# One token difference for both mixings on GpSimd, another order of snapshots and blocks 21 and 12, a low word read unsigned, and the w_k sums on VectorE

## The chip, the cores and the metric

The kernel runs on one core of a Trainium2 chip. The metric is the device time of one execution in microseconds, the median of three runs: 1744.05 us before (1743.65 to 1745.59).

## What is computed

A Fourier transform over tokens and features, of which the real part goes on, then a channel-mixing layer in which each token is mixed with the one before it, then a two-matrix layer with a tanh. All inputs are float32, the weights are handed in as 64-bit floats.

```python
X = np.fft.fft(np.fft.fft(x, axis=1), axis=2).real      # x: 4 x 3072 x 256
x_prev = concat([zeros, X[:, :-1]], axis=1)
xk = mu_k * X + (1.0 - mu_k) * x_prev
xr = mu_r * X + (1.0 - mu_r) * x_prev
k = np.maximum(xk @ w_k, 0.0)                           # 256 x 1024
v = k * k @ w_v                                         # 1024 x 256
r = 1.0 / (1.0 + np.exp(-(xr @ w_r)))
y = r * v
h = y @ w_in                                            # 256 x 2048
return (h - np.tanh(h)) @ w_out                         # 2048 x 256
```

## The kernel before

**Three stages.** `fft_phase` makes the transform of four batches and leaves it in the tiles y (two for each batch). Meanwhile it works through a list of small closures, three or four for each step, which turn the weights from 64-bit words into float32 with integer operations on VectorE (`convert`: 17 pieces here). Then `phase1` (12 passes of two 512-token tiles) computes the first layer, and `phase2` (12 passes) the second.

**Products.** A product is three matmuls of 512 columns (`mm3`): high by high, high by low, low by high, so each operand is a pair: a high half (a cast on ScalarE) and a low half (a subtraction). `split` writes such a pair. A Winograd-like scheme makes a 2x2 block product from seven products.

**A quad.** `quad` is the unit of both phases. A pass of phase 1 has four quads (n the pass, q the quad), one of phase 2 eight. In a quad TensorE makes seven left products (a11, a12, s2, s3, s1, a22, s4) in three PSUM banks X, Z and W. ScalarE copies X out three times on the way: the snapshots s1, s2, s3. From the sums come four blocks 11, 22, 21 and 12. Each goes through `bend` (relu on ScalarE, in phase 2 tanh), `gate` (on VectorE), `hi` (cast on ScalarE) and `lo` (subtraction on VectorE), and is then the moving operand of the second products (`second`, six matmuls for a block). Blocks 11 and 22 are finished in their own quad. Blocks 21 and 12 wait in `late`, and their nine steps run in the quad after it, as do the second products of all four blocks. In phase 1 a quad has 7 x 3 + 4 x 6 matmuls and 6 more for the gate r (`r_block`), 51 in all; in phase 2 it has 45. At the end of a pass `done` multiplies the four results by r on VectorE.

**Slots.** Each quad calls `fill` four times. A call runs the closures that stand in the table `slots` under the next number, so a pass of phase 1 has 16 slots. In them the inputs of the next pass are made: `mixed` builds xk and xr for four half tiles each, with a scaled copy on ScalarE (line 502) and a multiply-add on VectorE (line 504); `left` forms four sums on GpSimd (lines 485 to 488) and splits seven operands (cast on ScalarE, subtraction on GpSimd, lines 304 and 305). Eight pieces of w_out are converted in the slots from 88 on: seven VectorE instructions, a GpSimd sum and two DMAs each. Every engine runs its instructions in the order in which they are written, so an instruction that waits holds up all that stand behind it on its engine.

**w_k.** For the four pieces of w_k `quad_weights` casts on VectorE, subtracts the low halves on GpSimd, and forms four 128 x 128 sums t on GpSimd; a second cast on VectorE waits for these.

Of the kernel before, what the change touches and what calls it, by code (L numbers as in the profile page):

```python
# [9 lines left out]
I32 = mybir.dt.int32  # L10
PSUM = bass.MemoryType.PSUM
# [240 lines left out]
NP = 12  # L252
# [30 lines left out]
class Kernel:  # L283
# [24 lines left out]
    def convert(self, rows, done, room, add, fine=False):  # L308

        V = self.V  # L310
        ALU = mybir.AluOpType
        t = {}
        def load():
            t["raw"], t["more"] = room()
            for c, r in enumerate(rows):
                n = 512 // len(rows)
                self.nc.sync.dma_start(out=t["raw"][:, n * c:n * c + n, :].rearrange("p n t -> p (n t)"), in_=r)
        def step(k, j):
            if k == j == 0:
# [3 lines left out]
            ai, bi, si = (x.bitcast(I32) for x in (a, b, s))  # L323
# [12 lines left out]
            if k == 3:  # L336
                V.scalar_tensor_tensor(b, bi, 2.0 ** -51, s, op0=ALU.mult, op1=ALU.mult)
        steps = [lambda k=k, j=j: step(k, j) for k, j in ((0, 0), (0, 1), (1, 0), (1, 1), (2, 0), (2, 1))] if fine else [lambda k=k: (step(k, 0), step(k, 1)) for k in range(3)]
        return [load] + steps + [lambda: step(3, 0)], [lambda: add.tensor_add(t["a"], t["a"], t["b"])] + [lambda f=f: f(t["a"]) for f in done]

# [20 lines left out]
    def quad_weights(self, pool, out, first=None):  # L361

        t = []
        def sums(src):
            t.append(pool.tile([128, 4, 128], F32, tag="t4", name="t4"))
            b12, b11, b21, b22 = (src[:, 128 * k:128 * k + 128] for k in range(4))
            self.split(out[:, :, 0:3], src[:, 128:512].rearrange("p (k n) -> p k n", k=3), self.G, first)
            D = self.G
            D.tensor_sub(t[0][:, 0], b12, b11)
            D.tensor_sub(t[0][:, 2], b22, b12)  # L370
            D.tensor_sub(t[0][:, 1], b22, t[0][:, 0])
            D.tensor_sub(t[0][:, 3], b21, t[0][:, 1])
# [16 lines left out]
    def quad(self, ph, n, q, nq, S, W, w2, done, extra=None):  # L389
# [10 lines left out]
        ctile = lambda: self.act.tile([128, TOK], F32, tag="c", name="c", bufs=6)  # L400
# [12 lines left out]
        late = iter(p["late"] if p else ())  # L413
        def after(k):
            for _ in range(k):
                next(late, lambda: None)()
        self.odd ^= 1
        X, Z = bank(f"x{self.odd}", "x"), bank("z", "z")
        P(X, "a11", True)
# [6 lines left out]
        after(2)  # L426
        P(X, "s2", False)
        V.tensor_add(Z, Z, s1)  # L428
        after(1)
# [8 lines left out]
        r = extra(bank(f"x{1 - self.odd}", "r")) if extra else None  # L438
# [3 lines left out]
        self.fill()  # L442
        Wb = bank("w", "w")
        P(Wb, "s1", True)
        if r:
            r()
# [6 lines left out]
        self.second(p, "21")  # L453
        lo("22", Z)
        self.fill()
# [8 lines left out]
        def t12():  # L464
            st["t12"] = bend(st["c12"])
        late = [t21, c12, lambda: gate(X, X, st["t21"]),  # L466
                t12, lambda: hi("21", X), lambda: gate(st["c12"], st["c12"], st["t12"]),  # L467
                lambda: lo("21", X), lambda: hi("12", st["c12"]),
                lambda: lo("12", st["c12"])]
        self.pend = dict(n=n, q=q, nq=nq, m=M, w=w2, done=done, late=late)  # L470


    def unit(self, S, name, src, tag="S"):
        def f():
            pool, bufs = (self.sp, 11) if tag == "S" else (self.p2b, 3)
            S[name] = pool.tile([128, 2, TOK], F32R, tag=tag, name=name, bufs=bufs)
            self.split(S[name], src(), self.G)
        return f

    def left(self, S, raw, tag="S"):  # L480

        G = self.G
        u = {k: self.unit(S, k, lambda i=i: raw[i], "S" if k in ("a11", "a12", "a22", "s1") else tag)
# [47 lines left out]
    def k_tasks(self, n):  # L531
# [6 lines left out]
        return [get(j) for j in range(4)], self.left(self.S[n], raw)  # L538

    def r_task(self, n, t, c):  # L540
        st = []
        def f0():
            st.append(self.sp.tile([128, TOK], F32, tag="xt", name="xt", bufs=2))
            self.mixed(st[0], n, t, c, 1, 0)
        def f1():
            self.mixed(st[0], n, t, c, 1, 1)
        def f2():
            if c == 0:
                self.XR[n, t] = self.xp.tile([128, 2, 2, TOK], F32R, tag="xr", name="xr", bufs=2)
            self.split(self.XR[n, t][:, :, c], st[0], self.G if n + t else self.V)  # L550
        return [f0, f1, f2]

    def phase1(self):
# [26 lines left out]
        at = self.at  # L580
        for q in range(8):
            steps, out = self.convert(self.chunk_rows(self.w_out, (q, q + 8)), self.keep(12 + q), self.y_room, self.G, True)
            z = 91 + 11 * q
            at(z - 3, steps[0])
            at(z, *steps[1:], *out)
        for n in range(NP):
            z = 16 * n
            last = n + 1 == NP
            at(z if last else z + 4, *r_task(n, 1, 0))
            at(z + 1 if last else z + 6, *r_task(n, 1, 1))  # L590
            if n % 6 == 2:
                at(z + 8, lambda n=n: self.swap_rows(block(n, 1)[0]))
            if not last:
                get, u = self.k_tasks(n + 1)
                k = z + 1 if n else z + 2
                at(k, *get[0], u["a11"])
                at(k + 2, *get[1], u["a12"])
                at(k + 4, *get[3], u["a22"])
                at(k + 6, *get[2], u["+s1"], u["s1"])
                at(z + 10 if n else z + 11, u["+s3"], u["+s2"], u["+s4"], u["s3"], u["s2"], u["s4"])  # L600
                at(z + 10, *r_task(n + 1, 0, 0))
                at(z + 12, *r_task(n + 1, 0, 1))
                if n % 6 == 1:
                    at(z + 14, lambda n=n: self.swap_rows(block(n + 1, 0)[0]))
# [8 lines left out]
    def open2(self):  # L613
# [6 lines left out]
        for q in range(3):  # L620
            self.weights2(16 * NP - 12 + 4 * q, q, self.sp, "xt", 2)
# [34 lines left out]
    def phase2(self):  # L656
# [13 lines left out]
        for n in range(NP):  # L670
            for q in range(8):
                if n == 0 and q == 1:
                    self.xctx.close()
                    self.p2b = self.ctx.enter_context(self.tc.tile_pool(name="p2b", bufs=1, side="right", reuse_waits="tile"))
                    for j in range(3, 8):
                        self.weights2(z0 + 4 * (j - 2), j, self.sp, "xt", 2)
# [6 lines left out]
        for f in self.pend["late"]:  # L683
            f()
# [82 lines left out]
```

## Time and profile before

| | before |
|---|---|
| median of three runs | 1744.05 us |
| the profiled execution's own time | 1742.07 us |
| its span, first to last instruction | 1740.3 us |
| mean granted TensorE clock | 0.995 |
| TensorE busy (matmuls) | 1693.5 us, 97% |
| VectorE, ScalarE, GpSimd busy | 1335.9, 1191.9, 490.6 us |
| first matmul of phase 1, of phase 2 | 158.24 us, 747.53 us |

Matmuls are pipelined, so two that follow each other overlap in the record; how long a stretch takes is better read from how many matmuls were issued in it. An engine's busy share is an average over the stages.

### The profile page before, as it was taken

Reading aid. Unit: us, or ns where it says so; the run is one execution under the profiler, and the core shown is the slowest. Engines: PE = TensorE matmul, PEld = TensorE weight load, DVE = VectorE, ACT = ScalarE, POOL = GpSimd, SP = SyncE. Lnnn points to the kernel's source line nnn. Section 1 sums busy time; section 2 is a strip of 40 time slices with the busy share of each in tenths; the row PEclk is TensorE's granted clock in tenths of the full one; section 3 lists DMA queues with packets and bytes.
Section 4 is the critical chain, followed back from the end, with each engine's and each line's share of the span. In section 5 each row is a group of like instructions: output and inputs, shape, how many; then the busy total and the mean of one; then the engine's idle time right before and its main releaser. Section 6 shows DMA issues by size and latency. Waiting matters only on the chain.

```text
span 1740.3 us, 22465 instructions
## 1 busy us (share of the span) xinstructions
PE 1693.5 (97%) x7962; PEld 1408.9 (81%) x7962; DVE 1335.9 (77%) x2089; ACT 1191.9 (68%) x2368; POOL 490.6 (28%) x405
## 2 busy tenths in 40 slices
PE   9998999999999999999999999999999999999999
PEld 8897788888777777887888888888888888888887
DVE  6996788888888889776777777777777777777776
ACT  6657777777777677777666666666666666666665
POOL 0214444344344453557021111202020302021100
PEclk9999999999999999999999999999999999999999
DMA  9531000001111011221101010110101010101000
GB/s 338 171 94 43 1 25 26 25 24 37 43 43 62 19 43 43 91 80 31 49 1 49 1 49 8 42 42 8 49 1 49 1 49 1 49 1 49 1 25 25
DMA packets 37441, 77.64 MB, mean 45 GB/s; under 512 B 4288, under 2 KB 11072, under 8 KB 36176
## 3 DMA queue, kind: packets, MB, share of 16 engines
q1 hardware_dynamic: 37184, 76.21, 13.2%
q8 instruction: 62, 1.02, 0.2%
q14 instruction: 51, 0.42, 0.1%
q10 hardware_dynamic: 144, 0.00, 0.0%
HBM read 45.73 MB, written 30.46 MB: 44 GB/s over the span
## 4 chain that ended last, share of the span: by engine, by line
PE 68%; DVE 17%; ACT 8%; issue 3%; DMA 2%; POOL 1%; SPq 0%; DVEq 0%; ACTq 0%; POOLq 0%
PE o L272 12%; PE o L273 12%; PE o L271 12%; PE x L271 6%; PE x L272 6%; PE x L273 6%; PE w L273 3%; PE w L271 3%; PE w L272 3%; DVE m L411 3%; ACT c L404 2%; DVE xt L504 2%; ACT m L409 1%; PE z L273 1%; PE z L272 1%
## 5 line engine op out<-in xcount | busy, mean ns | idle before, releaser
L411 DVE TENSOR_TENSOR m<-z,m 128x512 fp32r<-128x512 f32 x288 | 199.1, 691 | 184.4 <-ACT m L409 184.4
L272 PE MATMUL o<-m,WO 128*128 128x512 f32 x768 | 298.9, 389 | 0.0
L273 PE MATMUL o<-m,WO 128*128 128x512 f32 x768 | 298.8, 389 | 0.0
L271 PE MATMUL o<-m,WO 128*128 128x512 f32 x768 | 298.8, 389 | 0.0
L409 ACT CAST m<-z 128x512 fp32r<-128x512 f32 x288 | 168.9, 586 | 165.2 <-DVE z L435 84.1
L305 POOL TENSOR_TENSOR a<-xk,a 128x512 fp32r<-128x512 f32 x72 | 95.4, 1326 | 640.1 <-ACT a L304 560.3
L404 ACT ACTIVATE c<-z 128x512 f32<-128x512 f32 x288 | 172.9, 600 | 132.5 <-DVE z L447 126.0
L305 POOL TENSOR_TENSOR s<-xk,s 128x512 fp32r<-128x512 f32 x96 | 128.7, 1342 | 243.5 <-ACT s L304 243.5
L272 PEld LDWEIGHTS o<-m,WO 128*128 128x128 f32 x768 | 144.2, 188 | 30.3 <-DVE m L411 0.3
L271 PEld LDWEIGHTS o<-m,WO 128*128 128x128 f32 x768 | 144.2, 188 | 29.9
L273 PEld LDWEIGHTS o<-m,WO 128*128 128x128 f32 x768 | 144.2, 188 | 29.9
L451 DVE TENSOR_TENSOR z<-z,c 128x512 f32<-128x512 f32 x144 | 100.3, 697 | 68.8 <-ACT c L404 68.8
L271 PE MATMUL o<-m,wv 128*128 128x512 f32 x384 | 149.6, 390 | 0.0
L273 PE MATMUL o<-m,wv 128*128 128x512 f32 x384 | 149.4, 389 | 0.0
L272 PE MATMUL o<-m,wv 128*128 128x512 f32 x384 | 149.4, 389 | 0.0
L422 ACT COPY s<-x 128x512 f32<-128x512 f32 x144 | 84.5, 587 | 73.2 <-PE x L273 73.0
L447 DVE TENSOR_TENSOR z<-w,s 128x512 f32<-128x512 f32 x144 | 100.5, 698 | 23.2 <-ACT r L569 5.8
L435 DVE TENSOR_TENSOR z<-z,c 128x512 f32<-128x512 f32 x144 | 100.5, 698 | 21.6 <-ACT c L404 19.5
L467 DVE TENSOR_TENSOR c<-c 128x512 f32<-128x512 f32 x96 | 71.2, 741 | 52.8 <-ACT c L404 52.8
L466 DVE TENSOR_TENSOR x<-x,c 128x512 f32<-128x512 f32 x144 | 99.1, 688 | 2.6 <-ACT c L404 2.6
L431 ACT COPY s<-x 128x512 f32<-128x512 f32 x144 | 84.6, 588 | 22.3 <-PE x L273 22.2
L428 DVE TENSOR_TENSOR z<-z,s 128x512 f32<-128x512 f32 x144 | 99.0, 688 | 0.0
(174 smaller groups left out, 4219.0 us busy)
## 6 DMA issues: line engine op xcount, KB each, us to landing
spill<-r SPq DMA_DIRECT2D x48, 256.0 KB
xk<-spill SPq DMA_DIRECT2D x48, 256.0 KB
out<-o SPq DMA_DIRECT2D x22, 512.0 KB
xr<-x SPq DMA_DIRECT2D x9, 1024.0 KB
raw<-w_in SPq DMA_DIRECT2D x32, 128.0 KB
cv<-w_out SPq DMA_DIRECT2D x16, 256.0 KB
wf<-wf SPq DMA_DIRECT2D x16, 256.0 KB
wf<-cva SPq DMA_DIRECT2D x12, 256.0 KB
```

Source lines behind the costliest of these rows:

```text
L271: T.matmul(ps, w[0], m[0], start=start, stop=False, skip_group_check=True)
L272: T.matmul(ps, w[0], m[1], start=False, stop=False, skip_group_check=True)
L273: T.matmul(ps, w[1], m[0], start=False, stop=stop, skip_group_check=True)
L305: eng.tensor_sub(out[:, 1], src, out[:, 0].bitcast(F32))
L404: A.activation(t, src, ACT.Tanh if ph == 2 else ACT.Relu)
L409: A.copy(M[blk][:, 0], g)
L411: V.tensor_sub(M[blk][:, 1], g, M[blk][:, 0].bitcast(F32))
L428: V.tensor_add(Z, Z, s1)
L435: gate(Z, Z, t11)
L447: V.tensor_add(Z, Wb, s3)
L451: gate(Z, Z, t22)
L466: late = [t21, c12, lambda: gate(X, X, st["t21"]), t12, lambda: hi("21", X), lambda: gate(st["c12"], st["c12"], st["t12"]), lambda: lo("21 ...
```

## The change

Four things change.

First, the mixing. Before, xk and xr of a half tile each took a scaled copy and a multiply-add, four instructions. Now (`both_tasks`) GpSimd forms one difference d = X - x_prev, VectorE makes xk = mu_k d + x_prev, ScalarE scales d by mu_r in place, and GpSimd adds x_prev to give xr. A dictionary says in which of the 16 slots each step stands (d, k, m, +, x for difference, xk, scaling, sum and split of half tile 0 to 3). The inputs of pass 0 keep the old way, but their sums and low halves go to VectorE.

Second, the quad of phase 1. The snapshot s2 is copied before block 12's relu and cast, block 21's second products come before the product s1, and block 12's after it. Phase 2 keeps its order.

Third, `convert` multiplies the low word straight as an unsigned integer, without the shift by one bit ahead of it. The w_out pieces are spread over 48 chosen slots of passes 6 to 9.

Fourth, the sums t of w_k are formed on VectorE. Buffers: c tiles 4 in place of 6, xt tiles 4 in place of 2.

```diff
-            if (k, j) == (2, 1):
-                V.tensor_scalar(bi, low, 1, None, op0=ALU.logical_shift_right)
             if k == 3:
-                V.scalar_tensor_tensor(b, bi, 2.0 ** -51, s, op0=ALU.mult, op1=ALU.mult)
+                V.scalar_tensor_tensor(b, low.bitcast(U32), 2.0 ** -52, s, op0=ALU.mult, op1=ALU.mult)
...
-            D = self.G
-            D.tensor_sub(t[0][:, 0], b12, b11)
+            eng.tensor_sub(t[0][:, 0], b12, b11)
...
         P(X, "a11", True)
-        after(3)
+        if ph == 1:
+            late("t21", "g21")
...
         s1 = stile()
         A.copy(s1, X)
-        after(3)
+        if ph == 1:
+            late("c12", "h21")
...
         A.copy(s2, X)
+        if ph == 1:
+            self.fill()
+            late("t12", "g12")
         t11 = bend(Z)
-        self.fill()
...
         gate(Z, Z, t11)
+        if ph == 1:
+            late("h12", "l12")
         P(X, "s3", False)
...
+        if ph == 1:
+            self.second(p, "21")
         Wb = bank("w", "w")
         P(Wb, "s1", True)
...
         hi("22", Z)
-        self.second(p, "21")
-        lo("22", Z)
-        self.fill()
+        if ph == 1:
+            self.fill()
+            lo("22", Z)
...
+                self.G.tensor_sub(d[j], t[:, cu:cu + TOK], y[j])
...
+                self.V.scalar_tensor_tensor(raw[j], d[j], self.mut[:, j % 2:j % 2 + 1], y[j], op0=ALU.mult, op1=ALU.add)
...
+            u[f"m{j}"] = lambda j=j: self.A.activation(d[j], d[j], ACT.Copy, scale=self.mut[:, 2 + j % 2:3 + j % 2])
+            u[f"+{j}"] = lambda j=j: self.G.tensor_add(d[j], d[j], y[j])
+            u[f"x{j}"] = lambda j=j: self.r_parts(n, j // 2, j % 2, d[j])
...
+        free = iter([16 * n + k for n in range(6, NP) for k in (0, 2, 3, 6, 7, 9, 10, 11, 12, 13, 14, 15)])
...
+                for k, names in {0: "d0", 1: "k0 d1", 3: "m0", 4: "k1 d3 a11", 5: "k3 +0", 6: "m1 d2 a12", 7: "+1", 8: "k2 m3 a22",
+                                 9: "+s1 m2", 10: "+3 s1 +s3", 11: "+s2 +2", 12: "s3 +s4", 13: "s2", 14: "s4", 15: "x0", 16: "x1", 18: "x2", 19: "x3"}.items():
```

How the instructions stand on the engines at three places:

VectorE in the transform stage, around the third piece of w_k, before (L333, L335 and L337 are the last three steps of `convert`, L304 the casts into TK, L217 and L219 write y).

```order
L339 TENSOR_TENSOR cva<-cva,cvb 128x512
L304 CAST TK<-cva 128x384
L217 TENSOR_TENSOR y_1_770<-pe,pq 128x12x16
L219 SCALAR_TENSOR_TENSOR y_1_770<-pq,cst,pe 128x12x16
L217 TENSOR_TENSOR y_1_771<-pe,pq 128x12x16
L219 SCALAR_TENSOR_TENSOR y_1_771<-pq,cst,pe 128x12x16
L333 TENSOR_SCALAR cvs<-cva 128x512
L335 TENSOR_SCALAR cvb<-raw 128x512
L337 SCALAR_TENSOR_TENSOR cvb<-cvb,cvs 128x512
```

The same place in the changed kernel.

```order
L338 TENSOR_TENSOR cva<-cva,cvb 128x512
L305 CAST TK<-cva 128x384
L367 TENSOR_TENSOR t_912<-cva 128x128
L368 TENSOR_TENSOR t_912<-cva 128x128
L369 TENSOR_TENSOR t_912<-cva,t_912 128x128
L370 TENSOR_TENSOR t_912<-cva,t_912 128x128
L218 TENSOR_TENSOR y_1_764<-pe,pq 128x12x16
```

The four sums now stand on VectorE right behind the cast; one of the three last steps of `convert` is gone everywhere.

ScalarE in phase 1, between two quads of pass 3, before (c the relus, m the high halves, L422 and L431 the snapshots s1 and s2, c<-w and m<-w those of block 12).

```order
L409 CAST m_3274<-z 128x512
L304 CAST a_3284<-xk 128x512
L502 ACTIVATE xk<-y_1_771,omu 128x512
L404 ACTIVATE c<-x 128x512
L422 COPY s<-x 128x512
L404 ACTIVATE c<-w 128x512
L409 CAST m_3308<-x 128x512
L409 CAST m_3321<-w 128x512
L431 COPY s<-x 128x512
```

The changed kernel, from the first to the second quad of pass 3 (L598 is m0, L424 and L439 the snapshots).

```order
L402 ACTIVATE c<-z 128x512
L305 CAST xr<-xt 128x512
L407 CAST m_3161<-z 128x512
L305 CAST xr<-xt 128x512
L598 ACTIVATE xt<-xt,mut 128x512
L402 ACTIVATE c<-x 128x512
L424 COPY s<-x 128x512
L407 CAST m_3184<-x 128x512
L439 COPY s<-x 128x512
```

Ahead of the snapshot s2 stand one relu and one high half fewer; ahead of block 21's relu stand the high half of block 22, a cast of xr and m0.

VectorE in the changed kernel, first quad of pass 2 (L593 is k0, L611 the products with r, L464 and L468 sum and gate of block 22, L409 low halves).

```order
L409 TENSOR_TENSOR m_2677<-z,m_2677 128x512
L593 SCALAR_TENSOR_TENSOR xk<-xt,mut,y_0_341 128x512
L611 TENSOR_TENSOR r<-o_2346,r 128x512
L611 TENSOR_TENSOR r<-o_2347,r 128x512
L464 TENSOR_TENSOR z<-w,s 128x512
L611 TENSOR_TENSOR r<-o_2316,r 128x512
L611 TENSOR_TENSOR r<-o_2317,r 128x512
L468 TENSOR_TENSOR z<-z,c 128x512
L409 TENSOR_TENSOR m_2726<-z,m_2726 128x512
```

GpSimd at the same place: the split of xr (x0 and x1), d0 and d1, then x2 and x3.

```order
L306 TENSOR_TENSOR xr<-xt,xr 128x512 x2
L588 TENSOR_TENSOR xt<-y_0_341 128x512
L588 TENSOR_TENSOR xt<-y_0_340 128x512
L306 TENSOR_TENSOR xr<-xt,xr 128x512 x2
```

Two of the four products with r, and k0, now stand ahead of the sum of block 22, and d1 follows d0 on GpSimd without a wait between them.

## Rows read from the trace of the kernel before

**Rows 1.** The page, part 1: busy time of each engine.

```profile
PE 1693.5 (97%) x7962; PEld 1408.9 (81%) x7962; DVE 1335.9 (77%) x2089; ACT 1191.9 (68%) x2368; POOL 490.6 (28%) x405
```

**Rows 2.** Windows: stretch, length, busy time (instructions) by engine, granted clock, DMA.

```profile
158.20:205.00 46.80, 38.67 (x162) 28.96 (x161) 33.80 (x53) 34.64 (x65) 20.51 (x16) 1.00 0.04 12
205.00:428.00 223.00, 221.15 (x969) 181.18 (x968) 181.31 (x268) 172.74 (x319) 92.25 (x71) 1.00 0.08 27
428.00:703.00 275.00, 257.46 (x1098) 204.79 (x1097) 238.32 (x355) 197.23 (x362) 126.22 (x92) 0.99 0.12 40
...
900.00:1000.00 100.00, 100.00 (x442) 82.80 (x442) 72.94 (x111) 64.57 (x118) 14.44 (x12) 1.00 0.07 22
```

**Rows 3.** Waits, 428 to 703 us: who waited for whom, us, times, longest.

```profile
PE x L271 <- ACT s L431: 16.5, 13, 2.2
```

**Rows 4.** VectorE's and ScalarE's timelines, quads of pass 3: start, us, instruction [idle before].

```profile
326.22 1.80 DVE L504 SCALAR_TENSOR_TENSOR xt<-y,mut,xt 128x512 f32<-128x512 f32 x1
...
330.51 0.59 ACT L431 COPY s<-x 128x512 f32<-128x512 f32 x1
...
336.26 0.73 ACT L502 ACTIVATE xt<-y,omu 128x512 f32<-128x512 f32 x1
...
344.98 0.69 DVE L411 TENSOR_TENSOR m<-z,m 128x512 fp32r<-128x512 f32 x1 [0.91 <-ACT m L409]
345.58 0.74 DVE L504 SCALAR_TENSOR_TENSOR xt<-y,mut,xt 128x512 f32<-128x512 f32 x1
346.24 0.69 DVE L447 TENSOR_TENSOR z<-w,s 128x512 f32<-128x512 f32 x1
347.60 0.70 DVE L451 TENSOR_TENSOR z<-z,c 128x512 f32<-128x512 f32 x1 [0.67 <-ACT c L404]
349.11 0.69 DVE L411 TENSOR_TENSOR m<-z,m 128x512 fp32r<-128x512 f32 x1 [0.81 <-ACT m L409]
```

**Rows 5.** GpSimd's timeline, same stretch.

```profile
326.17 1.30 POOL L305 TENSOR_TENSOR a<-xk,a 128x512 fp32r<-128x512 f32 x1 [0.40 <-ACT a L304]
```

**Rows 6.** TensorE's timeline, same stretch.

```profile
331.15 0.50 PE L271 MATMUL x<-s,TK 128*128 128x512 f32 x1 [0.37 <-ACT s L431]
...
345.39 0.39 PE L273 MATMUL w<-s,TK 128*128 128x512 f32 x1
...
351.74 0.39 PE L271 MATMUL z<-a,TK 128*128 128x512 f32 x1
```

**Rows 7.** Windows of the transform stage, same columns.

```profile
50.00:60.00 10.00, 10.00 (x91) 9.74 (x90) 9.83 (x20) 7.03 (x30) 0.60 (x1) 1.00 0.69 229
...
110.00:120.00 10.00, 6.67 (x48) 6.42 (x48) 9.76 (x24) 4.00 (x17) 1.16 (x1) 0.84 0.30 96
120.00:130.00 10.00, 10.00 (x76) 10.00 (x76) 9.72 (x23) 5.70 (x24) 1.27 (x1) 0.82 0.23 81
130.00:140.00 10.00, 8.80 (x76) 8.21 (x75) 9.79 (x26) 7.02 (x26) 0.00 (x0) 1.00 0.21 79
```

**Rows 8.** VectorE by line, 20 to 140 us: times, busy us, mean ns, idle before.

```profile
L335 DVE TENSOR_SCALAR cvb<-raw 128x512 int32<-128x512 int32 x17 | 9.8, 577 | 0.0
...
L217 DVE TENSOR_TENSOR y<-pe,pq 128x192 f32<-128x192 f32 x24 | 8.3, 347 | 0.0
...
L304 DVE CAST TK<-t 128x512 fp32r<-128x512 f32 x4 | 1.7, 426 | 4.2 <-POOL t L372 4.2
```

**Rows 9.** ScalarE's timeline at the end of the transform stage.

```profile
136.55 0.72 ACT L502 ACTIVATE xk<-y,omu 128x512 f32<-128x512 f32 x1 [1.79 <-DVE cvb L335]
```

**Rows 10.** VectorE's timeline, a first quad of a pass: products with r.

```profile
455.14 1.28 DVE L561 TENSOR_TENSOR r<-o,r 128x512 f32<-128x512 f32 x2
```

**Rows 11.** VectorE and GpSimd by line, 420 to 740 us, columns as above.

```profile
L331 DVE SCALAR_TENSOR_TENSOR cv<-cv,cv 128x512 int32<-128x512 int32 x8 | 7.9, 992 | 0.0
...
L327 DVE TENSOR_SCALAR cv<-cv 128x512 f32<-128x512 f32 x8 | 6.0, 754 | 0.0
...
L485 POOL TENSOR_TENSOR xk<-xk 128x512 f32<-128x512 f32 x7 | 9.1, 1297 | 0.1
```

More of the change, by code (lines that the diff above doesn't have):

```diff
@@ L322, in step @@
             a, b, s = (t[x] for x in "abs")
[L323 removed]
+            ai, si = (x.bitcast(I32) for x in (a, s))
             if (k, j) == (0, 0):
@@ L359, in chunk_rows, with quad_weights @@
         return [r[128 * c:128 * c + 128] for c in chunks]
-    def quad_weights(self, pool, out, first=None):
-        t = []
+    def quad_weights(self, pool, out, first=None, eng=None):
+        t, eng = [], eng or self.G
         def sums(src):
@@ L412, in quad, with late @@
         p, self.pend = self.pend, None
[L413 to L416, printed above, removed]
+        def late(*names):
+            for k in names:
+                if p:
+                    p["late"][k]()
         self.odd ^= 1
         X, Z = bank(f"x{self.odd}", "x"), bank("z", "z")
+        r = None
         P(X, "a11", True)
-        after(3)
+        if ph == 1:
+            late("t21", "g21")
+        else:
+            late("t21", "c12", "g21")
         s1 = stile()
         A.copy(s1, X)
-        after(3)
+        if ph == 1:
+            late("c12", "h21")
+        else:
+            late("t12", "h21", "g12")
         self.second(p, "11")
         P(Z, "a12", True)
-        after(2)
+        late("l21")
+        if ph == 2:
+            late("h12")
         P(X, "s2", False)
         V.tensor_add(Z, Z, s1)
-        after(1)
+        if ph == 2:
+            late("l12")
         s2 = stile()
         A.copy(s2, X)
+        if ph == 1:
+            self.fill()
+            late("t12", "g12")
         t11 = bend(Z)
-        self.fill()
+        if ph == 2:
+            self.fill()
         self.second(p, "22")
         gate(Z, Z, t11)
+        if ph == 1:
+            late("h12", "l12")
         P(X, "s3", False)
         hi("11", Z)
-        r = extra(bank(f"x{1 - self.odd}", "r")) if extra else None
+        if extra:
+            r = extra(bank(f"x{1 - self.odd}", "r"))
         s3 = stile()
@@ L537, in get @@
             return [f, lambda: self.mixed(raw[j], n, j // 2, j % 2, 0, 1)]
-        return [get(j) for j in range(4)], self.left(self.S[n], raw)
+        return [get(j) for j in range(4)], self.left(self.S[n], raw, eng=self.V)
     def r_task(self, n, t, c):
@@ L580, in phase1 @@
         at = self.at
+        free = iter([16 * n + k for n in range(6, NP) for k in (0, 2, 3, 6, 7, 9, 10, 11, 12, 13, 14, 15)])
         for q in range(8):
             steps, out = self.convert(self.chunk_rows(self.w_out, (q, q + 8)), self.keep(12 + q), self.y_room, self.G, True)
-            z = 91 + 11 * q
-            at(z - 3, steps[0])
-            at(z, *steps[1:], *out)
+            when = [next(free) for _ in steps[1:]]
+            at(when[0] - 4, steps[0])
+            for w, f in zip(when, steps[1:]):
+                at(w, f)
+            at(when[-1] + 1, *out)
         for n in range(NP):
             z = 16 * n
-            last = n + 1 == NP
-            at(z if last else z + 4, *r_task(n, 1, 0))
-            at(z + 1 if last else z + 6, *r_task(n, 1, 1))
+            if n == 0:
+                for t, (f0, f1, f2) in ((2, self.r_task(0, 1, 0)), (3, self.r_task(0, 1, 1))):
+                    at(t, f0, f1, f2)
             if n % 6 == 2:
[L592 to L602, printed above, removed]
+                at(z + 4, lambda n=n: self.swap_rows(block(n, 1)[0]))
+            if n + 1 < NP:
+                u = self.both_tasks(n + 1)
+                for k, names in {0: "d0", 1: "k0 d1", 3: "m0", 4: "k1 d3 a11", 5: "k3 +0", 6: "m1 d2 a12", 7: "+1", 8: "k2 m3 a22",
+                                 9: "+s1 m2", 10: "+3 s1 +s3", 11: "+s2 +2", 12: "s3 +s4", 13: "s2", 14: "s4", 15: "x0", 16: "x1", 18: "x2", 19: "x3"}.items():
+                    for name in names.split():
+                        at(z + k, u[name])
                 if n % 6 == 1:
-                    at(z + 14, lambda n=n: self.swap_rows(block(n + 1, 0)[0]))
+                    at(z + 12, lambda n=n: self.swap_rows(block(n + 1, 0)[0]))
             for q in range(4):
```

83 lines of the change are left out of this document (55 added, 28 removed).

## The prediction

> **What bounds the kernel now.** I read the page first: TensorE is busy 97% of the span, the others far less [rows 1]. That does not say that nothing is to be had, since overlapping matmuls count as busy. So I counted matmuls in windows [rows 2]. From 900 to 1000 us 442 are issued, one each 0.2262 us, with no gap: phase 2 is at TensorE's pace and only fewer matmuls would shorten it. From 205 to 428 us 969 x 0.2262 = 219.2 of 223 us are used, so 3.8 are lost; from 428 to 703 us 1098 x 0.2262 = 248.4 of 275, so 26.6 are lost; from 158.2 to 205 us 36.6 of 46.8, so 10.2. In the 26.6 VectorE is busy 238 of 275 us, where w_out is converted beside the normal work.
>
> The waits say what ends the losses there: TensorE waits for the snapshot s2 [rows 3]. The timelines show how [rows 4 to 6]. A multiply-add xt of VectorE takes 1.80 us from 326.22 where one takes 0.74 at 345.58, because GpSimd runs a two-input subtraction until 327.47; block 12's sum, relu, gate and cast follow, and behind that cast, in ScalarE's order, s2 is copied only at 330.51. The product s3 starts at 331.15, 0.37 late with a longer first matmul.
>
> In the transform stage [rows 7] VectorE is busy 9.7 to 9.8 of 10 us from 50 us on, and TensorE gets 48 matmuls in 110 to 120 us against 91 in 50 to 60. After that pause its granted clock is 0.84 and 0.82 over 110 to 130 us, a mean of stretches at 2.4 and at 1.2 GHz. The stage is bound by VectorE up to about 138 us, where ScalarE still waits 1.79 us for the conversion [rows 9]. After it ScalarE's copies set the pace.
>
> **The change, part by part.** *Transform stage.* The shift (L335) goes 17 times, of which I count 13 behind 50 us, where VectorE is full. It lasts 0.42 undisturbed (mean 0.577 with disturbed ones [rows 8]) and the next starts some 0.40 behind its start: 13 x 0.40 = 5.2 us. The multiply that now reads the low word with a stride and as unsigned has no row; L331 reads its high word with the same stride, undisturbed in the time of a contiguous one, so I take no change; were the conversion to halve its rate it would cost 0.6 x 13 = 8 us, which would turn this term's sign. The cast that waited for GpSimd's sums loses its wait, 4.2 us in four, three of them behind 50 us: 3.2. Twelve sums of 128 columns come to VectorE: 192 columns last 0.347 [rows 8] and overlap, so 0.22 each, 2.6; at 0.35 each 4.2. Sum 5.2 + 3.2 - 2.6 = 5.8, and some 1.2 from the early piece and from sums that no longer get in VectorE's way: 7 us. Above: all seventeen and all four count, 6.8 + 4.2 - 4 x 4 x 0.2 = 7.8, and the clock comes back over 110 to 130 us (20 x 0.17 = 3.4): 11. Below: the unsigned read eats it, -1. That the first pass's sums and low halves go to VectorE costs nothing as I see it: VectorE is free once the conversions end, and ScalarE's copies cover eleven instructions of 0.7 us; without that cover 2 us.
>
> *First four quads.* They lose 10.2 us. The new order takes s2's wait away, but VectorE gets k0 in front of block 22's sum (0.74, or 1.8 beside GpSimd's splits), and ScalarE gets m0 ahead of block 21. I take 0, between +2 and -3.
>
> *Quads of passes 1 to 11.* Each pass drops four scaled copies and four multiply-adds, and GpSimd gets eight instructions of 1.3 us [rows 11], 10.4 us in a pass of 46, on top of some 44 us in 100 (92.25 in 223 [rows 2]), so about two thirds busy: not a bound. TensorE's losses by s2 go, as s2 stands behind only one cast. What is late next? Three deadlines.
>
> The low half of block 22 frees bank Z. In [rows 4, 6] the last matmul of s1 starts at 345.39, the sum follows at 346.24, the low half ends at 349.80, and the next quad's a12 starts at 351.74: 1.94 to spare. Product s1 moves six matmuls, 1.36 us, back, so 0.58 is left. Enough in a plain quad.
>
> The first quad of a pass is not plain, as two of the products with r now stand ahead of that sum. I count from the quad's first product. A quad takes 51 x 0.2262 = 11.54 and a12 begins nine matmuls, 2.04, in, so the quad of [rows 4] began at 351.74 - 2.04 - 11.54 = 338.16, and block 11's low half ended 7.5 us in (345.67). With one more cast in front, 7.9. The split x1 waits for a cast that follows s2's snapshot (the product ends at 15 x 0.2262 = 3.4; snapshot and cast bring it to 4.7); x1, d0 and d1 follow each other on GpSimd at 1.3: d0 ends at 7.3 and d1 at 8.6. So k0 is issued at about 7.8 and stands behind d1 as xt stood behind GpSimd at 326.22; it ends about 9.1. Two products with r (1.28 [rows 10]): 10.2. Sum 0.69: 10.9. Relu beside two more products: 12.0. Gate 0.70: 12.7. High half: 13.3. ScalarE then has x3's cast (0.5), m0 (some 0.63 to the next start, as L502 at 336.26) and block 21's relu, to 14.9, and the snapshot s1, to 15.4. TensorE wants it for s2 at 11.54 + 12 x 0.2262 = 14.25. That is 1.2 us lost, in each of the ten passes that make inputs: 12. If k0 met no GpSimd work it would be 0.4; with a full block by d1, 2.
>
> The 48 conversion steps stand mostly where VectorE waits anyway, for relu (0.67) or cast (0.81) [rows 4]. One in a pass stands in the chain just told, 0.45 (0.41 to 1.5): four passes, 2. For two-input and two-port operations that meet GpSimd at other places (L331 took 0.992 on the mean, L327 0.754 [rows 11], undisturbed 0.69 and 0.41) I add 2. So 16 us lost where 3.8 + 26.6 = 30.4 were: 14 gained.
>
> **Sum.** 7 + 0 + 14 = 21 off the profiled execution's 1742.07: 1721.1. The median of the runs stands 1.98 above that execution, so 1723.
>
> What the Trainium skill says of this: "SBUF — State Buffer", Who interferes with whom, has VectorE with two SBUF inputs and a reading GpSimd instruction exclude each other for the whole instruction, whichever issued first going on. The 1.80 us row agrees. By it the 1.2 us above would hold in each pass, as I took it. "GPSIMD Engine Reference", Engine selection, advises against two-input work on GpSimd as about twice VectorE's time; 1.297 against 0.69 here agrees, and it speaks against eight more such instructions, though only where they are waited for.
>
> **Rivals.** *GpSimd shuts VectorE out.* With two thirds busy instead of four ninths, each conversion step and each k waits on the mean 0.6 more. 16 quads x 3 steps x 0.6 and 40 x 0.6 make 53 us of VectorE time; were a quarter of it on the path, 14 gained turn to 0: 1737. For it: mean 0.992 against 0.69 already. Against: most waits then fall into VectorE's own gaps. The Trainium skill's rule on SBUF, named above, is the one behind it.
>
> *No stalls left.* GpSimd's split runs earlier, k0 meets nothing, and passes lose 0.4: 4 us instead of 16, the transform gives 11, the first quads 3: 1744 - 40 = 1704. For it: the deadlines are missed by little, and the slots look spread over VectorE's gaps.
>
> *The transform gains nothing,* since the unsigned read or the sums cost what the shift gave: 1730.
>
> *Slower.* Bank Z misses in every quad. It has 0.58 us to spare; each us beyond is paid in 44 quads. With 30.4 + 7 us gained, it decides from 37.4 / 44 = 0.85 us a quad on, that is with 1.4 us more in the chain from s1 to block 22's low half than today. Two blocked instructions in each quad would do it; 1.2 a quad gives 1744 - 37 + 53 = 1760. Against: outside the first quad no GpSimd-exposed instruction stands in that chain.
>
> **How the numbers follow.** Forecast 0.47, no stalls 0.24, GpSimd 0.15, transform nothing 0.07, slower 0.07. The range 1703 to 1738 leaves out half of the no-stall case (0.12) and the slower one (0.07). A measurement of this kernel can tell some 0.2%, 3.5 us. Slower by more than that: 0.06 (the slower case, nearly all). Same: 0.05, the upper end of GpSimd's case and a little of the slower one. Faster: 0.89.
>
> **What would show it.** In the trace after, the first matmul of phase 1 stands at about 151 us instead of 158.24, no row has ScalarE waiting for a conversion, and the granted clock is nearer to 1 over 110 to 130 us. TensorE's wait for s2 is under 3 us; in its place a wait for the snapshot s1 appears once a pass, in the second quad, 1.2 us each, or for bank Z. From 205 us to phase 2 about 16 us are lost by the count. Phase 2 takes the same time. I am wrong if waits for Z or for W come in quads outside the first, or if the multiply with the unsigned low word lasts over 0.9 us.

## The result and the profile after

The changed kernel takes 1720.28 us (median of four runs, 1720.17 to 1720.44) against 1743.85 us in the same series (1742.58 to 1745.59): ratio 0.9864, 95% interval 0.9847 to 0.9881. The execution profiled after has a time of its own of 1720.17 us; the one before had 1742.07, so 21.9 us went between the two traces that are compared here.

The page after, part 1, as [rows 1]:

```profile
PE 1688.0 (98%) x7962; PEld 1407.4 (82%) x7962; DVE 1303.1 (76%) x2047; ACT 1163.4 (68%) x2324; POOL 566.0 (33%) x466
```

GpSimd's busy time rose from 28 to 33% of the span, VectorE's total fell by 33 us. Where the gain lies is read from the windows (columns as in [rows 2, 7]):

```profile
158.20:205.00 46.80, 40.76 (x168) 32.07 (x168) 34.37 (x50) 34.36 (x64) 31.43 (x24) 0.96 0.04 11
205.00:428.00 223.00, 220.97 (x964) 179.87 (x964) 164.42 (x249) 160.98 (x299) 134.08 (x108) 1.00 0.08 27
428.00:703.00 275.00, 271.97 (x1187) 221.42 (x1187) 231.81 (x349) 197.29 (x366) 180.22 (x143) 1.00 0.16 52
900.00:1000.00 100.00, 100.00 (x443) 82.80 (x442) 73.92 (x112) 66.28 (x121) 14.74 (x12) 1.00 0.14 43
...
110.00:120.00 10.00, 8.59 (x76) 8.47 (x76) 9.72 (x20) 5.90 (x24) 1.28 (x1) 1.00 0.36 106
120.00:130.00 10.00, 9.12 (x81) 8.75 (x81) 9.73 (x20) 6.48 (x25) 1.58 (x1) 1.00 0.15 54
130.00:140.00 10.00, 5.88 (x32) 5.49 (x32) 6.64 (x21) 5.43 (x15) 0.00 (x0) 0.75 0.14 52
...
136.00:138.00 2.00, 2.00 (x10) 1.80 (x10) 1.18 (x2) 1.96 (x6) 0.00 (x0) 0.50 0.00 0
...
142.00:144.00 2.00, 2.00 (x20) 2.00 (x19) 1.44 (x3) 1.54 (x5) 0.00 (x0) 1.00 0.04 8
```

Count matmuls as the prediction did, 0.2262 us each. From 428 to 703 us there are 1187 instead of 1098: 6.5 us lost instead of 26.6. From 205 to 428 us 964 instead of 969: 4.9 lost instead of 3.8. From 900 to 1000 us phase 2 is as it was. The passes lose 11.4 us where they lost 30.4, so nearly all of the gain is in the second stretch, the one in which w_out is converted.

The transform stage gained less than was forecast. From 110 to 130 us TensorE does 157 matmuls instead of 124, at full clock. Then 130 to 140 us has 32 where it had 76. The timeline shows why (ScalarE, VectorE and TensorE, columns as in [rows 4, 6, 9]):

```profile
131.60 0.69 DVE L338 TENSOR_TENSOR cva<-cva,cvb 128x512 f32<-128x512 f32 x1
...
128.15 0.20 ACT L167 ACTIVATE zt<-zt 64x2 f32<-64x2 f32 x1
134.47 0.72 ACT L522 ACTIVATE xk<-y,omu 128x512 f32<-128x512 f32 x1 [6.12 <-DMA wf<-cva]
...
135.51 0.74 PE L194 MATMUL pp<-cst,zt 128*128 128x96 f32 x2 [4.12 <-ACT zt L164]
...
155.73 0.47 PE L272 MATMUL x<-a,TK 128*128 128x512 f32 x1
...
724.53 0.39 PE L272 MATMUL x<-a,TI 128*128 128x512 f32 x1
```

The last conversion ends at 132.29 us (before: 137.97), and its result is sent to DRAM. ScalarE's second copy of the first pass waits 6.12 us for that transfer: its tile xk now lies on the tile that is being sent. Before, the second copy did not wait; the first had waited 1.79 us, for VectorE [rows 9]. By the addresses in the two programs the two tiles more of xt move xk by two tiles: the last conversion's tile was under the fourth xk tile, and is now under the second. The zt copies stand behind the waiting copy, TensorE idles 4.12 us, and from 136 us on its granted clock is 0.50, the 1.2 GHz level, until about 142 us. Phase 1 starts at 155.73 us, only 2.5 earlier than the 158.24 of before. Phase 2 starts at 724.53 us, 23.0 earlier.

### The profile page after: what moved, and what is told of

Same layout as the page of the kernel before. It is cut to its first block, busy times and chain, and to the rows that moved or that the text cites. A ratio compares the mean times of both kernels' runs of the same rounds, so it can differ in the third digit from the quotient of the medians.

```text
span 1718.4 us, 22470 instructions
## 1 busy us (share of the span) xinstructions
PE 1688.0 (98%) x7962; PEld 1407.4 (82%) x7962; DVE 1303.1 (76%) x2047; ACT 1163.4 (68%) x2324; POOL 566.0 (33%) x466
## 3 DMA queue, kind: packets, MB, share of 16 engines
q1 hardware_dynamic: 37184, 76.21, 13.3%
## 4 chain that ended last, share of the span: by engine, by line
PE 87%; DVE 7%; ACT 3%; DMA 2%; issue 1%; SPq 0%; DVEq 0%; ACTq 0%
PE o L273 15%; PE o L274 15%; PE o L272 15%; PE x L272 8%; PE x L274 7%; PE x L273 7%; PE w L272 4%; PE w L274 4%; PE w L273 4%; PE z L272 2%; PE z L273 2%; PE z L274 2%; PE r L273 1%; PE r L274 1%; PE r L272 1%
## 5 line engine op out<-in xcount | busy, mean ns | idle before, releaser
L409 DVE TENSOR_TENSOR m<-z,m 128x512 fp32r<-128x512 f32 x288 | 198.7, 690 | 143.7 <-ACT m L407 143.7
L306 POOL TENSOR_TENSOR s<-xk,s 128x512 fp32r<-128x512 f32 x92 | 122.1, 1328 | 236.6 <-ACT s L305 236.6
L468 DVE TENSOR_TENSOR z<-z,c 128x512 f32<-128x512 f32 x144 | 100.5, 698 | 72.0 <-ACT c L402 71.4
L439 ACT COPY s<-x 128x512 f32<-128x512 f32 x144 | 84.4, 586 | 64.3 <-PE x L274 64.2
L424 ACT COPY s<-x 128x512 f32<-128x512 f32 x144 | 84.6, 588 | 59.2 <-PE x L274 58.9
L464 DVE TENSOR_TENSOR z<-w,s 128x512 f32<-128x512 f32 x144 | 100.4, 697 | 30.8 <-PE w L274 17.9
L409 DVE TENSOR_TENSOR m<-x,m 128x512 fp32r<-128x512 f32 x144 | 98.8, 686 | 2.6
```

Source lines behind the costliest of these rows:

```text
L306: eng.tensor_sub(out[:, 1], src, out[:, 0].bitcast(F32))
L409: V.tensor_sub(M[blk][:, 1], g, M[blk][:, 0].bitcast(F32))
L464: V.tensor_add(Z, Wb, s3)
L468: gate(Z, Z, t22)
```

## The experiments

All times are medians of four or five runs; the kernel before ran between them, with medians of 1743.5 to 1744.6 us. "Lost" is the count from 428 to 703 us.

| run | us | against changed | phase 1 starts | matmuls, lost us |
|---|---|---|---|---|
| changed kernel | 1720.28 | | 155.73 | 1187, 6.5 |
| shift back | 1725.40 | +5.1 | 161.25 | |
| sums on GpSimd | 1723.24 | +3.0 | 157.56 | |
| xk moved | 1718.16 | -2.1 | 153.12 | |
| xk moved, first pass later | 1714.43 | -5.9 | 149.03 | |
| m0 later | 1714.42 | -5.9 | 156.10 | 1200, 3.6 |
| old order | 1720.89 | +0.6 | 155.79 | 1181, 7.9 |
| old mixing | 1736.99 | +16.7 | 154.16 | 1124, 20.8 |
| first quad rearranged | 1713.99 | -6.3 | 156.58 | |
| old order, m0 later | 1724.23 | +4.0 | 155.01 | 1172, 9.9 |
| additions on VectorE | 1728.98 | +8.7 | 156.31 | 1157, 13.3 |
| conversions adjacent | 1724.58 | +4.3 | 156.04 | 1167, 11.0 |
| best | 1704.84 | -15.4 | 149.45 | 1200, 3.6 |

### The transform stage, part by part

**The shift back.**

```
+ V.tensor_scalar(bi, low, 1, None, op0=ALU.logical_shift_right)   # not in phase 1
- V.scalar_tensor_tensor(b, low.bitcast(U32), 2.0 ** -52, s, ...)
+ V.scalar_tensor_tensor(b, bi, 2.0 ** -51, s, ...)
```

> The logical shift of the low word is back in the conversions of the transform stage (one VectorE instruction more in each of 17), all else as in the changed kernel. My theory: VectorE sets the pace of this stage, and the copy that now waits for the last conversion's transfer hangs directly on its end, so 13 x 0.40 = 5 us come back in full: about 1725, the last conversion ends at about 137 us instead of 132.3. Rival: the wait for the transfer had already taken back what the shift gave, and only its end matters little: 1720 to 1721.5.

1725.40 us, 5.1 more. ScalarE's timeline has the same wait, moved as a whole:

```profile
140.75 0.72 ACT L526 ACTIVATE xk<-y,omu 128x512 f32<-128x512 f32 x1 [5.84 <-DMA wf<-cva]
```

The shift (with the signed multiply that it feeds) is worth what 13 x 0.40 said, and it reaches the path because the copy hangs on the end of the conversions.

**The sums back on GpSimd.**

```
- self.quad_weights(self.cv, self.TK[q], V.tensor_copy, V)
+ self.quad_weights(self.cv, self.TK[q], V.tensor_copy)
```

> The sums of the four w_k conversions are back on GpSimd, all else as in the changed kernel. My theory: the cast on VectorE waits again for GpSimd, some 3 us, against 2.6 us of sums that leave VectorE: between 1720 and 1721.5, too little to be told from the changed kernel. Rival 1: the sums on VectorE cost more than the waits (12 x 0.35): 1718.5. Rival 2: all four waits of before come back in full and stand on the path: 1722 or more.

1723.24 us, 3.0 more (1.8 by the start of phase 1 in the profiled executions): the expectation was too low, rival 2 is nearest. VectorE by line, 20 to 140 us, first line, and for comparison the changed kernel's four sums:

```profile
L305 DVE CAST TK<-t 128x512 fp32r<-128x512 f32 x4 | 1.7, 427 | 6.0 <-POOL t L370 6.0
```

```profile
L368 DVE TENSOR_TENSOR t<-cva 128x128 f32<-128x128 f32 x4 | 3.6, 901 | 0.0
L370 DVE TENSOR_TENSOR t<-cva,t 128x128 f32<-128x128 f32 x4 | 1.9, 463 | 0.1
...
L367 DVE TENSOR_TENSOR t<-cva 128x128 f32<-128x128 f32 x4 | 1.1, 284 | 0.0
L369 DVE TENSOR_TENSOR t<-cva,t 128x128 f32<-128x128 f32 x4 | 1.1, 280 | 0.0
```

The waits on GpSimd are 6.0 us in this kernel where before had 4.2 [rows 8]. The sums on VectorE are not cheap either, 7.7 us of busy time for sixteen, but the last conversion ends 1.5 us later with GpSimd (133.82).

**xk and xt change places.** The two xt tiles of the first pass are allocated ahead of xk's. By the addresses xt then lies where xk lay, and xk four tiles higher: off the tile that is being sent, though still on other buffers of the conversions, not on free memory as the expectation below has it.

```
+ xt = [self.sp.tile([128, TOK], F32, tag="xt", name="xt", bufs=4) for _ in range(2)]
  get, u = self.k_tasks(0)
- self.r0, self.r1 = (self.r_task(0, 0, c) for c in range(2))
+ self.r0, self.r1 = (self.r_task(0, 0, c, xt[c]) for c in range(2))   # uses that tile
```

> The buffers of the mixing change places: xk lies where xt lay, on memory that no conversion uses, so the second copy of the first pass no longer waits for the last conversion's transfer. Nothing else changes. My theory: the 6.1 us wait at 134.5 us goes, but two groups later ScalarE's cast a waits for the multiply-add of VectorE, which stands behind the last conversion (133.5 us): of the 6 us about 2 to 3 come back, 1717.5 to 1718.5. Rival 1: the whole wait was the price, and the granted clock stays at 2.4 GHz: 1714. Rival 2: the wait hid behind something else: 1720.

1718.16 us: the size that my theory gave. The wait for the transfer is gone. In ScalarE's waits of 110 to 162 us stand the next one, for VectorE's multiply-add behind the last conversion, and a short one of a copy that still lies on a conversion's buffer:

```profile
ACT a L305 <- DVE xk L524: 3.0, 2, 2.1
...
ACT xk L522 <- DVE cva L338: 1.1, 1, 1.1
```

**The same, and the first pass two groups later.**

```
- at(-13, *get[0], u["a11"])
- at(-12, *get[1], u["a12"])
+ at(-13, get[0][0]); at(-12, get[1][0])
+ at(-11, get[0][1]); at(-10, get[1][1], u["a11"])      # the others likewise
```

> As the run in which xk and xt changed places (1718.2), and besides it the casts and sums of the first pass are issued two groups later in the tail of the transform stage, so that ScalarE does not reach the cast of xk before VectorE has finished the conversions. My theory: the 3.0 us that ScalarE still waits there for VectorE's xk go, TensorE keeps its clock, and phase 1 starts at about 150 us instead of 153.9: 1714 to 1715. Rival: the work only crowds the last groups, where ScalarE sets the pace, and the start stays at 153 to 154: 1718.

1714.43 us, as expected. The windows, columns as before:

```profile
130.00:140.00 10.00, 9.58 (x84) 9.22 (x83) 8.03 (x27) 9.45 (x29) 1.54 (x1) 1.00 0.15 55
140.00:150.00 10.00, 9.22 (x74) 8.63 (x74) 8.53 (x17) 8.96 (x28) 0.00 (x0) 1.00 0.16 52
```

84 matmuls instead of 32 from 130 to 140 us, clock 1.00 throughout, and phase 1 starts at 149.03 us. This is the 7 us of the prediction and a little more: 158.24 - 149.03 = 9.2. The later first pass was run only together with the moved xk.

### The passes: mixing, order, spreading

**The old order with the new mixing.** Phase 1's late steps and blocks stand as before the change (for instance block 12's cast ahead of the snapshot s2, block 12 ahead of 21).

```
- if ph == 1:
-     late("t21", "g21")
- else:
-     late("t21", "c12", "g21")
+ late("t21", "c12", "g21")          # and so at each place of the order
```

> Phase 1 runs in the order of before (block 12's relu, gate and casts ahead of the snapshot s2, block 12 ahead of 21), the mixing by differences and all else as in the changed kernel. My theory: the new order took the waits for s2 away, and with the old one TensorE waits for s2 again in most quads, though the mixing asks less of VectorE than before: passes lose some 20 us where 12 are lost now and 30 were, 1726 to 1730. Rival: the mixing alone freed VectorE, the order matters little: 1720 to 1722.

1720.89 us: the rival is right and my theory wrong, as long as nothing else changes (a later run qualifies it). Windows and TensorE's waits of 428 to 703 us:

```profile
205.00:428.00 223.00, 222.97 (x975) 181.80 (x973) 166.31 (x250) 164.29 (x301) 135.29 (x109) 1.00 0.08 27
428.00:703.00 275.00, 271.29 (x1181) 220.05 (x1180) 227.89 (x347) 200.21 (x363) 182.91 (x142) 1.00 0.16 52
```

```profile
PE x L272 <- ACT s L439: 3.5, 4, 0.9
```

L439 is the snapshot s2: TensorE waits for it four times instead of thirteen, 3.5 us instead of 16.5 [rows 3], with its old place in ScalarE's order. So it was not the place of s2 that took the 13 us away.

**The old mixing in the new order.** Eight scaled copies and eight multiply-adds in a pass, in the places of before.

```
- u = self.both_tasks(n + 1)         # and its table of slots
+ get, u = self.k_tasks(n + 1, self.G)
+ at(k, *get[0], u["a11"]) ...; at(z + 10, *r_task(n + 1, 0, 0)) ...
```

> The mixing of before (eight scaled copies and eight multiply-adds in a pass, none on GpSimd, in the places of before), in the new order of phase 1, all else as in the changed kernel. My theory: the waits for s2 stay away, but VectorE's multiply-adds meet GpSimd's splits and stand ahead of sums: 1722 to 1727. Rival: the order alone brought the gain of the passes, and the mixing by differences with its m0 ahead of s1 rather costs: 1715 to 1719.

1736.99 us, ten above the upper end of my theory: from 428 to 703 us 20.8 us are lost again, in the new order. TensorE's waits and the timelines of one place in them:

```profile
PE z L272 <- DVE m L409: 8.5, 12, 1.2
```

```profile
476.91 1.52 DVE L328 TENSOR_SCALAR cv<-cv 128x512 f32<-128x512 f32 x1
478.35 1.78 DVE L524 SCALAR_TENSOR_TENSOR xt<-y,mut,xt 128x512 f32<-128x512 f32 x1
480.05 0.68 DVE L409 TENSOR_TENSOR m<-z,m 128x512 fp32r<-128x512 f32 x1
...
480.78 0.50 PE L272 MATMUL z<-a,TK 128*128 128x512 f32 x1 [1.18 <-DVE m L409]
```

The multiply-add takes 1.78 us, as the one at 326.22 of [rows 4] took 1.80, and a conversion step 1.52. Behind them stands the low half of block 22, which frees bank Z. Only the victim is another: bank Z instead of s2.

**Only the four additions back on VectorE.**

```
- u[f"+{j}"] = lambda j=j: self.G.tensor_add(d[j], d[j], y[j])
+ u[f"+{j}"] = lambda j=j: self.V.tensor_add(d[j], d[j], y[j])
```

> The additions of the mixing that makes the r inputs (four in a pass) run on VectorE instead of GpSimd, all else as in the changed kernel. It tells whether the passes gained because VectorE has four instructions fewer or because of what ScalarE and GpSimd do otherwise. Theory VectorE: with its eight mixing instructions back, the passes with conversions lose again, 1726 to 1732, and TensorE's waits for the low half of block 22 (bank z) rise over 5 us. Rival: VectorE has room for four more, the four scaled copies less on ScalarE and the slots brought the gain: 1719 to 1722.

1728.98 us, 8.7 more, as the theory of VectorE's load said; half of the 16.7 that the whole mixing is worth. Most of it is lost where w_out is converted (1157 matmuls instead of 1187); from 205 to 428 us there are 965, as in the changed kernel. What the other half consists of (the four scaled copies less, the places in the table) was not divided. VectorE's timeline has the same pattern with the addition in it:

```profile
480.10 1.77 DVE L599 TENSOR_TENSOR xt<-xt,y 128x512 f32<-128x512 f32 x1
481.79 0.68 DVE L409 TENSOR_TENSOR m<-z,m 128x512 fp32r<-128x512 f32 x1
```

**The conversion steps adjacent again.**

```
- for w, f in zip(when, steps[1:]):   # w from the table of free groups
-     at(w, f)
+ at(91 + 11 * q, *steps[1:], *out)
```

> The steps of the eight w_out conversions stand in adjacent groups again, at the places of before (five groups in a row from 91 + 11 q on), all else as in the changed kernel. It tells what the spreading over groups brought, since the run with the old mixing lost 20 us in these four passes although its conversions were spread. My theory: with the mixing by differences VectorE has the room, and adjacent steps cost little: 1721 to 1724. Rival: spreading and mixing work only together, and most of the 15 us of these passes comes back: 1730 to 1735.

1724.58 us, 4.3 more: just above the upper end of my theory. The spreading is worth a quarter of what the mixing is.

### What the passes still lose

Each pass still loses mainly at one place, the second quad. TensorE's, VectorE's, ScalarE's and GpSimd's timelines of the changed kernel, and TensorE's wait for s1 from 205 to 703 us:

```profile
348.17 0.39 PE L272 MATMUL z<-a,TK 128*128 128x512 f32 x1
...
359.81 0.50 PE L272 MATMUL z<-a,TK 128*128 128x512 f32 x1
...
361.18 0.50 PE L272 MATMUL x<-s,TK 128*128 128x512 f32 x1 [0.40 <-ACT s L424]
...
372.20 0.39 PE L272 MATMUL z<-a,TK 128*128 128x512 f32 x1
...
353.98 0.83 DVE L593 SCALAR_TENSOR_TENSOR xk<-xt,mut,y 128x512 f32<-128x512 f32 x1
...
355.93 0.68 DVE L464 TENSOR_TENSOR z<-w,s 128x512 f32<-128x512 f32 x1
...
358.44 0.59 ACT L407 CAST m<-z 128x512 fp32r<-128x512 f32 x1 [0.63 <-DVE z L468]
358.93 0.62 ACT L305 CAST xr<-xt 128x512 fp32r<-128x512 f32 x1
359.44 0.72 ACT L598 ACTIVATE xt<-xt,mut 128x512 f32<-128x512 f32 x1
360.07 0.59 ACT L402 ACTIVATE c<-x 128x512 f32<-128x512 f32 x1
360.55 0.58 ACT L424 COPY s<-x 128x512 f32<-128x512 f32 x1
...
352.22 2.04 POOL L588 TENSOR_TENSOR xt<-y 128x512 f32<-128x512 f32 x2
...
PE x L272 <- ACT s L424: 4.1, 10, 0.4
```

From 359.81 to 372.20 us are 12.39 us for 51 matmuls (11.54): 0.85 lost. From block 22's cast on ScalarE does x3's cast, m0, block 21's relu and then s1 (L424), one behind the other, and s2's product, which goes into the bank that s1 copies, waits for it: 0.40 us idle, the rest of the 0.85 in longer steps between the matmuls around it.

**m0 one group later.**

```
- 3: "m0", 4: "k1 d3 a11"
+ 4: "m0 k1 d3 a11"
```

> ScalarE's first scaled difference of a pass (m0) moves from the last slot of the first quad to the first slot of the second, so it no longer stands ahead of block 21's relu and the snapshot s1. My theory: the 0.87 us that the second quad of each of ten passes loses is the late s1, and 0.6 of it goes: 10 x 0.6 = 6 us, 1714 to 1715, and TensorE's waits for s1 fall from 5.2 us to under 1. Rival: the chain by GpSimd and bank Z sets it (the low half of block 22 is late too), and at most 1 us goes: 1719.5.

1714.42 us: 5.9 less. The wait for s1 is not in TensorE's list of this run.

**The first quad rearranged.** m0 and x3's cast later still, and in the first quad of all k0 and the low halves of the first two r inputs behind block 22's sum.

```
- self.at(1, lambda: (self.r0[2](), self.r1[2]()))
+ self.at(2, lambda: (self.r0[2](), self.r1[2]()))     # k0 of the first pass: 1 -> 2
```

> As the run with m0 one slot later (1714.4), and besides: m0 yet one slot later (the sum behind it too), the cast of x3 one slot later, and in the first quad of all k0 and the splits of the first r inputs go behind the sum of block 22. My theory: in that first quad TensorE's wait of 3.2 us for z goes, and the rest of the wait for s1 (0.2 in each of ten passes): 1709 to 1711. Rival: in the first quad the next link (the gate or the low half) is as late, and nothing more comes than m0's 6 us: 1713.5 to 1714.5.

1713.99 us, no more than m0 alone: the rival. VectorE and TensorE, and last k0 and the wait of the changed kernel at this place:

```profile
165.11 2.92 DVE L306 TENSOR_TENSOR xr<-xt,xr 128x512 fp32r<-128x512 f32 x2 [1.17 <-ACT xr L305]
...
169.95 0.69 DVE L409 TENSOR_TENSOR m<-z,m 128x512 fp32r<-128x512 f32 x1
...
170.70 0.80 PE L272 MATMUL z<-a,TK 128*128 128x512 f32 x1 [3.71 <-DVE m L409]
...
163.77 1.75 DVE L593 SCALAR_TENSOR_TENSOR xk<-xt,mut,y 128x512 f32<-128x512 f32 x1
...
166.19 0.79 PE L272 MATMUL w<-s,TK 128*128 128x512 f32 x1 [3.16 <-DVE z L464]
```

The wait of 3.16 us for z's sum became one of 3.71 for z's low half, one link on. What had to go was the work, not its place.

**The old order with m0 and x3 later.**

```
old order as above, and
- 3: "m0", 5: "k3 +0", 6: "m1 d2 a12", 19: "x3"
+ 5: "k3 m0", 6: "+0 m1 d2 a12", 20: "x3"
```

> The order of before in phase 1 with the new mixing (1720.9), and m0 and the cast of x3 later as in the best version. The theory that held in the runs before (the mixing by differences brought the gain of the passes, the order almost nothing; what is left is m0 and x3 ahead of the snapshots): the second quads fall from 0.54 to 0.1 us lost, those of the four passes with conversions from 1.6 to about 0.6, 1714.5 to 1715.5, no worse than the new order with m0 later. Rival: the old order keeps s2 behind block 12's cast, which is late by itself, and the loss stays: 1719 to 1721.

1724.23 us: beyond the rival, and 3.3 worse than the old order by itself. ScalarE and VectorE:

```profile
361.25 0.60 ACT L402 ACTIVATE c<-w 128x512 f32<-128x512 f32 x1 [0.89 <-DVE w L484]
...
363.10 0.59 ACT L439 COPY s<-x 128x512 f32<-128x512 f32 x1
...
367.32 1.76 DVE L593 SCALAR_TENSOR_TENSOR xk<-xt,mut,y 128x512 f32<-128x512 f32 x1 [0.35 <-POOL xt L588]
```

In the old order s2 stands behind block 12, whose relu waits for VectorE's sum: taking m0 from ScalarE brings little. By the starts of a12 the second quad of this pass loses 0.38 us where the old order by itself lost 0.52. And x3 later makes GpSimd's next difference late, which k3 waits for; the third quad now loses 0.55 where it lost 0.02. So with m0 and x3 both later the new order is worth some 10 us (1714.0 against 1724.2), and next to nothing as the change has it. The old order with m0 alone later was not run, so how much of the 10 is x3's is open.

**The best version:** xk moved, the first pass later, m0 and x3 later, and the low halves of the first two r inputs on GpSimd.

```
- self.split(self.XR[n, t][:, :, c], src, self.G if n + t else self.V)
+ self.split(self.XR[n, t][:, :, c], src, self.G)
```

> What has paid so far put together: xk off the conversions' memory and the first pass two groups later (1714.4 by itself), m0 and the cast of x3 later (m0 alone 1714.4 by itself), and the low halves of the first two r inputs on GpSimd, so that VectorE reaches the first quad's sum of block 22 sooner. My theory: the two gains are in different stages and add, 1708 to 1709, and the first quad's wait of 3.2 us for z goes, 2 to 3 us more: 1705 to 1707. Rival: in the first quad another link is as late, as in the run before: 1708.5.

1704.84 us, ratio 0.9779 to the kernel before (0.9764 to 0.9793). The windows:

```profile
205.00:428.00 223.00, 223.00 (x980) 183.16 (x980) 162.01 (x250) 163.76 (x302) 136.71 (x111) 1.00 0.08 27
428.00:703.00 275.00, 273.67 (x1200) 223.98 (x1199) 233.29 (x352) 199.80 (x370) 183.36 (x147) 1.00 0.17 54
```

980 and 1200 matmuls are 221.7 and 271.4 us: 4.9 lost in all the passes. The runs with one part each gave 5.9 and 5.9 to 6.3; the 3 us and more that are over may be the low halves on GpSimd, which were not run by themselves.

## Why the prediction held, and where it did not

The total, 21 us off, came out as 21.9, by errors that cancel and one wrong attribution: so close a hit is luck. The forecast of the median, 1723, was 2.7 too high. The three parts below, counted as in the prediction, give 2.5 + 1.4 + 19.0 = 22.9, and phase 2 does start 23.0 us earlier. It then takes 1.1 us longer than before (1718.4 - 724.53 = 993.9 against 1740.3 - 747.53 = 992.8), where the prediction set no change; about half of that is lost in its first quad.

*Transform stage, 7 forecast, 2.5 measured.* On VectorE the sum held: the last conversion ends 5.7 us earlier, where 5.8 was set. The unsigned multiply took 0.69 us at every step of this stage, as the signed one, so the bound of 8 us fell (beside GpSimd in phase 1 it takes 1.23 on the mean, 0.68 at the least); the shift is worth 5.1 by its run. Waits and sums together brought 1.8 to 3.0 instead of 0.6, though a sum took 0.48 us on the mean and not 0.22. What failed is the sentence that ScalarE's copies cover what follows and that no row has ScalarE waiting for a conversion: I followed the instructions and not the memory. The numbers of buffers were in the diff, and I priced them at nothing. The new wait for the transfer, and behind it the one for VectorE's xk, took the difference: by the starts of phase 1 the shift is worth 161.25 - 155.73 = 5.5 and the sums 1.8, 7.3 together, of which 2.5 arrived. The two runs that avoid the wait get 2.6 and 6.7 of it back.

*First four quads, 0 forecast.* From 158.2 to 205 us 168 x 0.2262 = 38.0 of 46.8 are used, 8.8 lost instead of 10.2: within the bounds of +2 and -3. VectorE's k0 in front of block 22's sum was foreseen, 1.75 us long beside GpSimd; with the two low halves of r inputs ahead of it (1.29) it makes the wait of 3.16 us, of which the best version, with these on GpSimd, has 0.53 left.

*Passes, 14 forecast, 19.0 by the same count.* The chain that I set as the next deadline is there, once a pass, in the place and with the length told. From the quad's first product, 2.04 us ahead of 348.17, k0 ends at 8.7 (9.1 forecast), block 22's sum at 10.5 (10.9), its high half at 12.9 (13.3), s1 at 15.0 (15.4), against 14.25 when it is wanted. It costs 0.85 instead of 1.2 us, since GpSimd's differences took 1.04 us and not 1.3: d1 ended at 8.1 instead of 8.6, so k0 lasted 0.83 and was barely held. Ten times 0.85 are 8.5 where 12 were set, and conversion steps and contention have 11.4 - 8.5 = 2.9 where 4 were set.

The wrong step is the attribution: "The new order takes s2's wait away". With the old order and the new mixing that wait falls from 16.5 to 3.5 us all the same, and with the new order and the old mixing 20.8 us are lost from 428 to 703 us. What I read from [rows 4, 5] was right, that a multiply-add of 0.74 us takes 1.80 beside GpSimd and delays what follows. The cure was the mixing, not the place of s2: four such instructions less on VectorE are half of what it is worth, and the other half was not divided.

*Rivals.* GpSimd did not shut VectorE out, though it is busy 314 us in 498 instead of 218 (44 in 100 before, as the prediction says, over both stretches; 92.25 in 223 alone are 41). It does hold VectorE: the 40 instructions k last 0.95 us on the mean where 0.74 is undisturbed. Little of it is on the path outside the first two quads of a pass: by the starts of a12 the third and fourth lose under 0.1 us. The rival without stalls set 4 us for the passes, where 11.4 are lost; the best version, with 4.9, stands at its 1704. Bank Z was not missed behind any quad but a first one: TensorE waits for it four times from 205 to 703 us, 1.0 us in all, each time for the first quad of a pass with conversions.

The Trainium skill's "GPSIMD Engine Reference", Engine selection, sends elementwise work to VectorE as twice as fast there. The additions take 1.29 us on GpSimd and 0.68 undisturbed on VectorE, which agrees, and yet the kernel is 8.7 us faster with them on GpSimd, where no row has an engine waiting for them. The Trainium skill's "SBUF — State Buffer", Who interferes with whom, has a VectorE instruction with two inputs in SBUF and a GpSimd instruction that reads SBUF shut each other out; the rows of 1.78, 1.77 and 2.92 us agree.

Open: what the remaining half of the mixing's 16.7 us is made of; some 0.4 us more in the first quads of the passes with conversions; 2 us in the first pass of phase 2, which both kernels lose, and the 1.1 us more of phase 2. These were not tried, nor were c's two buffers less and the first pass's sums on VectorE taken back by themselves.

## What to carry to other kernels

Ask of every change in the number of buffers what lies on that memory in the stage before, and who read it last: a transfer that sends a tile away holds it longer than the engine that made it, here by 2.2 us. Where one engine's instructions were delayed by another's, fewer of them helped in either order, while reordering only moved the wait to the next deadline until the work itself was out of the chain. And check a right total by taking its parts away one by one: here the largest part had the wrong reason.

## What was not expected of the hardware

GpSimd's plain differences of y (L588) take 1.04 us, where its two-input subtractions of xk tiles (L506) take 1.30; two rows of one shape and type, and no run shows why they differ. A sum of 128 columns on VectorE takes 0.28 us undisturbed, but the second of the four takes 1.10 in three of the four pieces:

```profile
57.42 1.10 DVE L368 TENSOR_TENSOR t<-cva 128x128 f32<-128x128 f32 x1
```

GpSimd's low half starts just ahead of it, at 57.38 us, and lasts 1.00: a short instruction is held just as a long one is. And 4.12 us without matmuls at 131 to 135 us were followed by some 6 us at a granted clock of 0.50.
